# Moving elementwise work between VectorE and GpSimd, and reordering the end of a token block, in an attention + MoE kernel

## Chip, cores and metric

The kernel runs on one NeuronCore of a Trainium2 chip. The metric is the device time of one execution in microseconds (us), lower is better. Engines are named as the profile names them: PE is TensorE (PEld its weight loads), DVE is VectorE, ACT is ScalarE, POOL is GpSimd, SP is SyncE, whose queue issues nearly all DMAs.

## What is computed

Three stages run one after the other: attention with a top-32 mask, a gated MLP, and a soft mixture of eight experts. The change touches only the third:

```python
def _moe2_ref(x, w_gate, w1, w2):          # x: 2304 x 512, w1: 8 x 512 x 1024, w2: 8 x 1024 x 512
    logits = x @ w_gate
    logits = logits - logits.max()
    P = np.exp(logits)
    for _ in range(8):
        P /= P.sum(1, keepdims=True) + 1e-09
        P /= P.sum(0, keepdims=True) + 1e-09
        P *= N / E
    out = np.zeros((N, D), dtype=np.float32)
    for e in range(E):
        h = np.maximum(x @ w1[e], 0.0)
        ye = h @ w2[e]
        out += P[:, e:e + 1] * ye
```

All is float32. The kernel feeds the PE with pairs of fp32r numbers: a high part (a rounded copy, written by ACT) and a low part (the number less its high part, one two-input subtraction on DVE or POOL), so that each product is three matmuls: high x high, high x low, low x high.

## The kernel before

**Blocks and units.** The third stage cuts the 2304 tokens into three blocks of 768 (each two halves of 384), and the hidden width of each of the 8 experts into four strips: 32 units a block, 96 in all. A product of 2x2 blocks is done with seven products of sums of the quarters instead of eight (a Winograd scheme). `l1` (lines 1152 to 1187) lists the seven products of the first matrix, i0 to i6, in the order `CH` = 6, 1, 4, 2, 0, 3, 5. Each is 6 matmuls of 384 columns. ACT copies product 6 out of PSUM as `p` (line 1178), DVE adds `p` and the running sums `u`, `c` to the others (L1162, L1165), ACT takes the high part of the rectified result, `hh` (L1169), and DVE the low part `hl` (L1170). PE runs ahead by at most a step or two: product 4 is accumulated on the bank of product 6 and so waits until ACT has copied `p`, and product 2 waits in the same way for `u`.

**First block** (time 809 to 1345). After each of i1 to i6 comes `l2` of the unit before, 6 matmuls of 512 columns, whose result DVE adds to `acc` (L1214). In the same loop all that the later blocks need is made:

- `w_load` (945) loads the raw quarters of the first weight matrix of the unit after the next into `ws`, two buffers. `w_sums` (953, the operation on 957) makes four more quarters as sums and differences of them, one instruction of 128x256 in each of i3 to i6. `w_split` (964) makes the high part (ACT, 967) and the low part (POOL, 968) of one quarter for the next unit, `wa`, and stores it (970) for the later blocks.
- `w2_load`, `w2_split` (980) and `w2_more` (994) do the same for the second matrix: `wb` (984), sums `sm` (1002) on DVE, parts `sp` (1006, 1007).
- A list of `steps`, one popped in each i by `slot()` (1228): first the 16 row and column normalizations of P on DVE (`rows` and `cols`, with one matmul for each column sum), then from unit 6 on the x of blocks three and two (`x_ops`, 1021): loads, sums `xr` (1037), and 28 pairs of high part (ACT, 1047) and low part (POOL, 1048) in `both`.

**Second and third block.** Units go through `d1` (1350). Products 1 to 7 of the hidden quarters with the second matrix (`group`, 1413) run for two units at a time, as pairs, and are spread over the i of the next two units by the list `todo2`; `take` (1428) adds each into `M1` to `M7` on DVE. Their PSUM banks go by chains: 1 and 2 share one, 5 and 3, and 7, 6 and 4. `KO` = 1, 2, 5, 3, 7, 6, 4 is the order. What `d1` still owes of a unit when its seven products are done, the list `late` of four functions, is run in i0 to i3 of the next unit: t2 and then t4 (two subtractions on POOL), and the high and low parts of hidden quarters 5, 7, 6 and 4. In the second block `v_make` (1330) also makes, for every second unit, the parts of the second matrix anew from `wr`, with four sums on DVE (1338) a unit: 60 instructions.

**End of a block.** The last pair has no next unit. `finish` (1466) runs its products at once, in the order 1, 5, 3, 7, 6, 4, 2, with the `late` parts in between. `plus` (1439) adds one M to another over its two halves, and `out_cols` (1443) transposes and stores a quarter of the output. Three additions are run before it in the last unit, in i3 and i5 (`early`, 1497).

**Order.** Scheduling is manual: on each engine instructions run in the order in which the code emits them, and an instruction that waits holds everything behind it on its engine.

Of the kernel before, what the change touches and what calls it, by code (L numbers as in the profile page):

```python
# [18 lines left out]
def kernel(  # L19
# [932 lines left out]

    def w_sums(e, u, part=None):
        st = wts[e, u]
        ops = ((0, 7, 3, ALU.add), (1, 0, 6, ALU.subtract), (2, 6, 7, ALU.subtract), (5, 4, 1, ALU.subtract))
        for dst, x, y, op in ops if part is None else ops[part:part + 1]:
            nc.vector.tensor_tensor(st[:, dst], st[:, x], st[:, y], op)  # L957

# [62 lines left out]
    def x_ops(s):  # L1021
# [24 lines left out]
        def both(c, b):  # L1046
            nc.scalar.activation(xB[b][:, 0, c], cur[c][:, b], AF.Copy)
            nc.gpsimd.tensor_tensor(xB[b][:, 1, c], cur[c][:, b], xB[b][:, 0, c].bitcast(F32), ALU.subtract)

# [215 lines left out]
    for n in range(NW):  # L1265
        e, u = units[n][1:]
        ops = l1(n)
        nxt = units[n + 1][1:]
        nx2 = units[n + 2][1:]
        if n == 6:  # L1270
            steps += x_ops(2) + p_steps() + x_ops(1)
        for i, fn in enumerate(ops):
            fn()
            if n and i:
                l2(n - 1, i - 1)
            run_after()
            (w_split if n + 1 < NW else w_fetch)(*nxt, CH[i])
            if n + 2 < NW:
                if i == 0:
                    w_load(*nx2)  # L1280
                if 3 <= i:
                    w_sums(*nx2, part=i - 3)
            if stores:
                stores.pop(0)()
            if more and i != 3:
                more.pop(0)()
            if i == 3:
                w2_split(e, u)
                if n + 1 < NW:
                    w2_load(*nxt)  # L1290
                if n % 2 == 0 or n == 1:
                    more = w2_more(e, u)
            if n < 6 or i not in (3, 4):
                slot()
# [35 lines left out]
    def v_make(n, k):  # L1330
# [6 lines left out]
        for dst, x, y, op in sums:  # L1337
            nc.vector.tensor_tensor(dst, x, y, op)
        t = wk2[n % 2][k]
# [10 lines left out]
    def d1(n):  # L1350
# [50 lines left out]

        def j0():
            G_.tensor_tensor(t["t2"], t["b22"], t["t1"], ALU.subtract)
            G_.tensor_tensor(t["b21"], t["b21"], t["t2"], ALU.subtract)
            parts(5, t["t1"], G_)

        return ([i0, i1, i2, i3, i4, i5, i6],
                [j0, lambda: parts(7, t["t3"], G_), lambda: parts(6, t["t2"], G_),
                 lambda: parts(4, t["b21"], G_)])

    bank = {}

    def group(pair, k, j, first=False):

        first = first or k in (1, 5, 7)
        if first:
            bank[CHAIN[k], j] = yps.tile([128, 512], F32, name="y", tag="y")
# [9 lines left out]

    def take(pair, k, j, *dst, first=False):
        ps = group(pair, k, j, first)
        for x in dst:  # L1430
# [35 lines left out]
    def finish(s, pair, late):  # L1466
# [4 lines left out]

        run(1, 1, 2)
        late.pop(0)()
        plus(3, 6, G_)
        plus(5, 1, V)
        run(5, 5)
        for fn in late:
            fn()
        plus(3, 1, V)
        run(3, 3)  # L1480
        plus(4, 1, V)
        run(7, -3)
        run(6, 5, 3)
# [6 lines left out]
        out_cols(s, 1, 0, 0, M[4][:, 0], M[1])  # L1490
        take(pair, 2, 0, 2, first=True)
        out_cols(s, 1, 0, 1, M[4][:, 1], M[1])
        take(pair, 2, 1, 2, first=True)
        out_cols(s, 0, 0, 0, M[2][:, 0], M[5])
        out_cols(s, 0, 0, 1, M[2][:, 1], M[5], V)

    early = {3: (3, 7, G_, ALU.subtract), 5: (5, 6, G_, ALU.add)}
    todo2 = []
# [66 lines left out]
```

## Time and profile before

| | us |
|---|---|
| Median of 3 runs (2335.92 to 2339.11) | 2338.88 |
| The profiled execution's own time | 2338.49 |
| Its span, first to last instruction | 2336.7 |
| PE busy in the span | 2217.1 (95%) |
| DVE busy | 1881.6 (81%) |
| POOL busy | 1444.1 (62%) |
| ACT busy | 1193.7 (51%) |
| Mean granted PE clock | 0.979 of 2.4 GHz |

The span is made of the attention and the MLP (until about 809), the first block (809 to 1345), the second (to 1850) and the third (to the end). Busy time is the sum of instruction durations; an instruction that is held up while it runs counts as busy. "Idle before" is the time in which an engine stood still before an instruction, with what ended it.

### The profile page before, as it was taken

The page shows a single profiled execution, that of the slowest core. Times are in us where ns is not written, and L with a number is a line of the kernel's source. Part 1 is how long each engine was busy: PE and PEld are TensorE (multiplying, and loading weights), DVE is VectorE, ACT ScalarE, POOL GpSimd, SP SyncE. Part 2 cuts the span into 40 slices and gives each one's busy share as a digit, 9 for nine tenths or more (in the row PEclk, how much of TensorE's full clock was granted, in tenths as well). Part 3 has the DMA queues.
Part 4 walks back from the last instruction along what each step waited for, and adds up shares of the span by engine and source line. Part 5 has one row for each costly group of instructions (what it writes and reads, how often), then busy time and mean ns, then how long its engine had stood idle before and what let it go on. Part 6 is the DMA issues. An engine that isn't in the chain of part 4 may idle for free.

```text
span 2336.7 us, 42305 instructions
## 1 busy us (share of the span) xinstructions
PE 2217.1 (95%) x13466; PEld 2021.8 (87%) x13466; DVE 1881.6 (81%) x4556; ACT 1193.7 (51%) x2705; POOL 1444.1 (62%) x1686
## 2 busy tenths in 40 slices
PE   5897999999999989999999999999999899999998
PEld 4555898888888877888788899999999899999998
DVE  8999899999896488988798867777777667777777
ACT  8999787787776343443433343333333343332232
POOL 6889776776774254766765546666666544444444
PEclk7997999999999999999999999999999999999999
DMA  6554444544540376787767687778778887777774
GB/s 188 150 148 117 106 109 110 123 98 110 125 110 22 127 245 208 249 292 248 241 236 238 236 298 260 270 264 278 269 270 273 298 281 255 257 260 255 258 256 145
DMA packets 352062, 483.88 MB, mean 207 GB/s; under 512 B 94976, under 2 KB 161888, under 8 KB 351840
## 3 DMA queue, kind: packets, MB, share of 16 engines
q1 hardware_dynamic: 350704, 479.34, 64.2%
q8 instruction: 108, 1.77, 0.3%
q10 hardware_dynamic: 1136, 1.84, 0.2%
q14 instruction: 114, 0.93, 0.1%
HBM read 307.90 MB, written 132.43 MB: 188 GB/s over the span
## 4 chain that ended last, share of the span: by engine, by line
PE 44%; DVE 4%; DMA 2%; issue 1%; POOL 1%; ACT 1%; SPq 0%; ACTq 0%; DVEq 0%; POOLq 0%
PE l1ps L1147 21%; PE y L1423 19%; PE y L1203 3%; DMA wr<-in_moe_w_dram 1%; DVE ws L957 1%; DMA ws<-in_moe_w_dram 1%; DVE acc L1214 0%; DVE sm L1002 0%; DVE l1ps L1361 0%; ACT h L1364 0%; DVE h L1365 0%; DVE hl L1170 0%; POOL wa L968 0%; DVE l1ps L1165 0%; DVE l1ps L1358 0%
## 5 line engine op out<-in xcount | busy, mean ns | idle before, releaser
L1423 PE MATMUL y<-h,v 128*128 128x384 f32 x2688 | 550.0, 340 | 7.8 <-POOL h L1365 6.0
L1147 PE MATMUL l1ps<-xB,wa 128*128 128x384 f32 x2688 | 541.1, 338 | 5.2 <-DVE tm_u L1358 5.0
L1423 PEld LDWEIGHTS y<-h,v 128*128 128x128 f32 x2688 | 482.1, 189 | 13.3 <-POOL h L1365 6.7
L1147 PEld LDWEIGHTS l1ps<-xB,wa 128*128 128x128 f32 x2688 | 471.3, 188 | 11.3 <-DVE tm_u L1358 9.2
L968 POOL TENSOR_TENSOR wa<-ws,wa 128x256 fp32r<-128x256 f32 x217 | 169.4, 788 | 208.2 <-ACT wa L967 201.4
L1437 DVE TENSOR_TENSOR M<-y,M 128x384 f32<-128x384 f32 x424 | 229.8, 553 | 79.9 <-PE y L1423 79.3
L1147 PE MATMUL l1ps<-xAh,wa 128*128 128x384 f32 x896 | 266.3, 344 | 27.9 <-ACT p L1178 16.2
L1203 PE MATMUL y<-wb,hh 128*128 128x512 f32 x768 | 272.5, 397 | 0.0
L1365 POOL TENSOR_TENSOR h<-tm_t,h 128x384 fp32r<-128x384 f32 x192 | 197.8, 1045 | 51.2 <-ACT h L1364 51.2
L1147 PEld LDWEIGHTS l1ps<-xAh,wa 128*128 128x128 f32 x896 | 165.2, 188 | 51.7 <-ACT p L1178 25.1
L1365 POOL TENSOR_TENSOR h<-tm_b,h 128x384 fp32r<-128x384 f32 x128 | 132.5, 1039 | 123.4 <-ACT h L1364 117.1
L315 POOL TENSOR_TENSOR low<-s_sb 128x288 int32<-128x288 int32 x144 | 117.6, 817 | 98.1 <-ACT s_sb L293 96.4
L338 DVE MAX8 tkv<-rest 128x8 f32<-128x288 f32 x432 | 175.2, 448 | 0.0
L1203 PEld LDWEIGHTS y<-wb,hh 128*128 128x128 f32 x768 | 145.9, 190 | 25.6
L1364 ACT ACTIVATE h<-tm_b 128x384 fp32r<-128x384 f32 x128 | 67.1, 524 | 188.2 <-DVE tm_b L1361 182.1
L289 PE MATMUL sps<-kst,qst 128*128 128x288 f32 x640 | 131.4, 334 | 33.3 <-DVE top L322 32.2
L1214 DVE SCALAR_TENSOR_TENSOR acc<-y,P,acc 128x512 f32<-128x512 f32 x168 | 123.7, 742 | 47.6 <-PE y L1203 42.9
L1341 POOL TENSOR_TENSOR v<-wr,v 128x256 fp32r<-128x256 f32 x105 | 80.3, 765 | 129.2 <-ACT v L1340 114.4
L1364 ACT ACTIVATE h<-l1ps 128x384 fp32r<-128x384 f32 x128 | 62.8, 490 | 184.0 <-DVE l1ps L1361 182.8
L1203 PE MATMUL y<-wb,hl 128*128 128x512 f32 x384 | 152.8, 398 | 0.0
L1147 PE MATMUL l1ps<-xAl,wa 128*128 128x384 f32 x448 | 150.5, 336 | 0.0
L289 PEld LDWEIGHTS sps<-kst,qst 128*128 128x128 f32 x640 | 100.9, 203 | 56.5 <-DVE top L322 44.8
(205 smaller groups left out, 5344.8 us busy)
## 6 DMA issues: line engine op xcount, KB each, us to landing
wa<-wk SPq DMA_DIRECT2D x448, 256.0 KB, 3.3
v<-vk SPq DMA_DIRECT2D x343, 256.0 KB, 3.7
wk<-wa SPq DMA_DIRECT2D x224, 256.0 KB, 2.6
vk<-v SPq DMA_DIRECT2D x105, 256.0 KB, 2.6
vk<-sp SPq DMA_DIRECT2D x68, 256.0 KB, 3.0
raw<-in_moe_w_dram SPq DMA_DIRECT2D x32, 512.0 KB, 3.8
ws<-in_moe_w_dram SPq DMA_DIRECT2D x128, 128.0 KB, 2.5
ws<-in_moe_w_dram SPq DMA_DIRECT2D x32, 512.0 KB, 4.6
```

What stands on the lines that cost most here:

```text
L289: nc.tensor.matmul(ps[:, e, 0:SH], lhs, kst[p, part][:, hh, SH * e:SH * e + SH], start=(n == 0), stop=(n == len(terms) - 1))
L315: nc.gpsimd.tensor_tensor(low_sb[st][:, j].bitcast(I32), x[:, 0:SH], x[:, SH:S], ALU.add)
L338: nc.vector.max(vt[:, j, c:c + 8], x[:, j])
L968: eng.tensor_tensor(t[:, 1], st[:, c], t[:, 0].bitcast(F32), ALU.subtract)
L1147: nc.tensor.matmul(ps, lhs[:, kc], rhs[:, kc], start=(first and k_ == 0), stop=(k_ == 3 * KH - 1), skip_group_check=True)
L1203: nc.tensor.matmul(ps, lhs[:, m, h, o:o + 128], rhs[:, m], start=(k_ == 0), stop=(k_ == 5))
L1214: nc.vector.scalar_tensor_tensor(a, ps, P[:, i, e:e + 1], a, op0=ALU.mult, op1=ALU.add)
L1341: nc.gpsimd.tensor_tensor(t[:, 1], src, t[:, 0].bitcast(F32), ALU.subtract)
L1364: nc.scalar.activation(h[k][:, 0], src, AF.Copy)
L1365: low = lambda: eng.tensor_tensor(h[k][:, 1], src, h[k][:, 0].bitcast(F32), ALU.subtract)
L1423: nc.tensor.matmul(ps, w[:, a, 128 * j:128 * j + 128], h[:, b], start=(first and q_ == 0), stop=(q_ == 5), skip_group_check=True)
L1437: nc.vector.tensor_tensor(m, ps, m, ALU.add)
```

## The change

Four parts:

1. `w_sums` takes an engine, and the first block's loop gives it POOL: 120 sums (30 units, 4 each) go from DVE to POOL. The two calls ahead of the loop stay on DVE.
2. In `both`, the 28 low parts of x go from POOL to DVE.
3. In `v_make`, the 60 sums go from DVE to POOL.
4. `late` is cut in another way: the part of quarter 5 first, then t2 with the part of 7, then t4 with the part of 6. `finish` runs 1, 3, 5, 7, 6, 4, 2; product 1 goes into two banks of its own (`far`, from the pool of the first matrix's products), and product 2 is accumulated on them; the additions among the M are rearranged.

```diff
-    def w_sums(e, u, part=None):
+    def w_sums(e, u, part=None, eng=None):
...
-            nc.vector.tensor_tensor(st[:, dst], st[:, x], st[:, y], op)
+            (eng or V).tensor_tensor(st[:, dst], st[:, x], st[:, y], op)
...
-            nc.gpsimd.tensor_tensor(xB[b][:, 1, c], cur[c][:, b], xB[b][:, 0, c].bitcast(F32), ALU.subtract)
+            nc.vector.tensor_tensor(xB[b][:, 1, c], cur[c][:, b], xB[b][:, 0, c].bitcast(F32), ALU.subtract)
...
-                    w_sums(*nx2, part=i - 3)
+                    w_sums(*nx2, part=i - 3, eng=G_)
...
-            nc.vector.tensor_tensor(dst, x, y, op)
+            nc.gpsimd.tensor_tensor(dst, x, y, op)
...
-        def j0():
+        def t2():
             G_.tensor_tensor(t["t2"], t["b22"], t["t1"], ALU.subtract)
+
+        def t4():
             G_.tensor_tensor(t["b21"], t["b21"], t["t2"], ALU.subtract)
-            parts(5, t["t1"], G_)
...
-                [j0, lambda: parts(7, t["t3"], G_), lambda: parts(6, t["t2"], G_),
-                 lambda: parts(4, t["b21"], G_)])
+                [lambda: parts(5, t["t1"], G_), lambda: (t2(), parts(7, t["t3"], G_)),
+                 lambda: (t4(), parts(6, t["t2"], G_)), lambda: parts(4, t["b21"], G_)])
...
-        if first:
+        if far:
+            bank[CHAIN[k], j] = lps.tile([128, 512], F32, name="z", tag="l1")
+        elif first:
...
-        run(1, 1, 2)
-        late.pop(0)()
-        plus(3, 6, G_)
-        plus(5, 1, V)
-        run(5, 5)
+        for j in range(2):
+            take(pair, 1, j, 1, far=True)
         for fn in late:
             fn()
+        for j in range(2):
+            take(pair, 3, j, 3, first=True)
+        run(5, 5, 3)
+        plus(4, 1, G_)
+        plus(5, 1, V)
+        run(7, -3)
         plus(3, 1, V)
-        run(3, 3)
-        plus(4, 1, V)
-        run(7, -3)
         run(6, 5, 3)
...
-        take(pair, 2, 0, 2, first=True)
+        take(pair, 2, 0, 2)
...
-        take(pair, 2, 1, 2, first=True)
+        take(pair, 2, 1, 2)
...
-    early = {3: (3, 7, G_, ALU.subtract), 5: (5, 6, G_, ALU.add)}
+    early = {3: (3, 7, G_, ALU.subtract), 4: (5, 6, G_, ALU.add), 5: (3, 6, G_, ALU.add)}
```

On ACT and on SP no instruction changes its place. Three places of the order, with the change's line numbers where rows are new:

POOL in the first unit of the first block, i3 to i6 (`ws` holds the raw quarters and their sums):

```order
 L968 TENSOR_TENSOR wa_10853<-ws_10371,wa_10853 128x256
+L957 TENSOR_TENSOR ws_10814<-ws_10814 128x256
 L984 TENSOR_TENSOR wb<-ws_10803,wb 128x1024
 L968 TENSOR_TENSOR wa_10875<-ws_10371,wa_10875 128x256
+L957 TENSOR_TENSOR ws_10814<-ws_10814 128x256
 L968 TENSOR_TENSOR wa_10899<-ws_10371,wa_10899 128x256
+L957 TENSOR_TENSOR ws_10814<-ws_10814 128x256
 L1007 TENSOR_TENSOR sp<-sm_10881,sp 128x256
 L968 TENSOR_TENSOR wa_10922<-ws_10371,wa_10922 128x256
+L957 TENSOR_TENSOR ws_10814<-ws_10814 128x256
```

Each sum now stands behind a low part, the first ahead of the long `wb` part of the second matrix.

DVE at the first of four runs of seven low parts of x (`xr` is x, `xB` its parts), i5 of one unit to i1 of the next:

```order
-L957 TENSOR_TENSOR ws_12167<-ws_12167 128x256
+L1048 TENSOR_TENSOR xB_10796<-xr,xB_10796 128x384
 L1165 TENSOR_TENSOR l1ps<-l1ps,u_12187 128x384
 L1214 SCALAR_TENSOR_TENSOR acc<-y,P,acc 128x512
 L1170 SCALAR_TENSOR_TENSOR hl<-l1ps,hh 128x384
-L957 TENSOR_TENSOR ws_12167<-ws_12167 128x256
+L1048 TENSOR_TENSOR xB_10793<-xr,xB_10793 128x384
+L1048 TENSOR_TENSOR xB_10795<-xr,xB_10795 128x384
 L1162 TENSOR_TENSOR u_12364<-l1ps,p_12343 128x384
-L1214 SCALAR_TENSOR_TENSOR acc<-y,P,acc 128x512 x2
-L1170 SCALAR_TENSOR_TENSOR hl<-l1ps,hh 128x384
+L1214 SCALAR_TENSOR_TENSOR acc<-y,P,acc 128x512
```

Sums are gone; the low parts stand where POOL had them in time, each behind the unit's own `hl`.

DVE in `finish` of the third block, before (`M5_16787` and the like are M5, M1, M3, M4; `y` banks 26643 and 26651 hold products 5 and 3, 26683 and 26691 product 7):

```order
L1441 TENSOR_TENSOR M5_16787<-M5_16787,M1_16785 128x384 x2
L1437 TENSOR_TENSOR M5_16787<-y_26643,M5_16787 128x384
L1437 TENSOR_TENSOR M5_16787<-y_26651,M5_16787 128x384
L1441 TENSOR_TENSOR M3_16788<-M3_16788,M1_16785 128x384 x2
L1437 TENSOR_TENSOR M3_16788<-y_26643,M3_16788 128x384
L1437 TENSOR_TENSOR M3_16788<-y_26651,M3_16788 128x384
L1441 TENSOR_TENSOR M4_16791<-M4_16791,M1_16785 128x384 x2
L1433 TENSOR_TENSOR M3_16788<-M3_16788,y_26683 128x384
L1433 TENSOR_TENSOR M3_16788<-M3_16788,y_26691 128x384
```

The same place in the change (`y` banks 26661 and 26670 hold product 5):

```order
L1440 TENSOR_TENSOR M5_16787<-y_26661,M5_16787 128x384
L1440 TENSOR_TENSOR M3_16788<-y_26661,M3_16788 128x384
L1440 TENSOR_TENSOR M5_16787<-y_26670,M5_16787 128x384
L1440 TENSOR_TENSOR M3_16788<-y_26670,M3_16788 128x384
L1444 TENSOR_TENSOR M5_16787<-M5_16787,M1_16785 128x384 x2
L1436 TENSOR_TENSOR M3_16788<-M3_16788,y_26683 128x384
L1436 TENSOR_TENSOR M3_16788<-M3_16788,y_26691 128x384
L1444 TENSOR_TENSOR M3_16788<-M3_16788,M1_16785 128x384 x2
L1440 TENSOR_TENSOR M5_16787<-y_26683,M5_16787 128x384
```

The subtraction of product 7 (L1433 before, L1436 now), which must be over before product 6 can be accumulated on its bank, stands behind one pair of M additions instead of three since product 1; the pair for M3 follows it and the one for M4 is on POOL.

## Rows read from the trace of the kernel before

**Rows 1.** By stretch: us, busy PE PEld DVE ACT POOL, PEclk, DMA share, GB/s.

```profile
810.00:960.00 150.00, 133.46 (x647) 115.44 (x646) 131.38 (x240) 62.75 (x147) 86.11 (x92) 0.98 0.67 229
960.00:1190.00 230.00, 216.47 (x1049) 187.66 (x1048) 197.23 (x298) 92.60 (x224) 154.45 (x160) 0.99 0.74 257
1190.00:1320.00 130.00, 128.95 (x638) 113.81 (x637) 115.00 (x173) 50.79 (x122) 75.68 (x81) 1.00 0.71 242
```

**Rows 2.** The same view, inside the second block.

```profile
1440.00:1800.00 360.00, 358.24 (x2016) 352.35 (x2016) 274.28 (x528) 135.75 (x324) 234.56 (x252) 1.00 0.79 270
```

**Rows 3.** Waits from 840 to 1350: waiter <- awaited: us, times, longest.

```profile
PEld l1ps L1147 <- ACT p L1178: 21.7, 20, 2.4
```

**Rows 4.** Timeline of VectorE around one stop: start, us, what.

```profile
859.63 0.90 DVE L957 TENSOR_TENSOR ws<-ws 128x256 f32<-128x256 f32 x1
860.46 0.96 DVE L1002 TENSOR_TENSOR sm<-sm,ws 128x256 f32<-128x256 f32 x1
861.34 0.55 DVE L1165 TENSOR_TENSOR l1ps<-l1ps,u 128x384 f32<-128x384 f32 x1
```

**Rows 5.** Timeline of ScalarE, same place.

```profile
861.93 0.49 ACT L1169 ACTIVATE hh<-l1ps 128x384 fp32r<-128x384 f32 x1 [2.19 <-DVE l1ps L1165]
...
862.93 0.48 ACT L1178 ACTIVATE p<-l1ps 128x384 f32<-128x384 f32 x1
```

**Rows 6.** Timeline of TensorE, same place.

```profile
863.46 0.44 PE L1147 MATMUL l1ps<-xAh,wa 128*128 128x384 f32 x1 [1.79 <-ACT p L1178]
```

**Rows 7.** VectorE by group, 810 to 1340: xcount | busy us, mean ns.

```profile
L957 DVE TENSOR_TENSOR ws<-ws 128x256 f32<-128x256 f32 x120 | 125.8, 1048 | 18.9 <-DMA ws<-in_moe_w_dram 17.3 <-POOL wa L968 1.5
...
L1170 DVE SCALAR_TENSOR_TENSOR hl<-l1ps,hh 128x384 fp32r<-128x384 f32 x93 | 50.9, 548 | 7.1 <-ACT hh L1169 7.1
...
L1170 DVE SCALAR_TENSOR_TENSOR hl<-c,hh 128x384 fp32r<-128x384 f32 x31 | 22.5, 725 | 1.3 <-ACT hh L1169 1.3
...
L1037 DVE TENSOR_TENSOR xr<-xr 128x384 f32<-128x384 f32 x16 | 13.8, 867 | 0.7 <-DMA xr<-x2s 0.7
```

**Rows 8.** GpSimd by group, same stretch.

```profile
L968 POOL TENSOR_TENSOR wa<-ws,wa 128x256 fp32r<-128x256 f32 x217 | 169.4, 788 | 208.2 <-ACT wa L967 201.4 <-DMA vk<-sp 2.7 <-DMA ws<-in_moe_w_dram 2.7
...
L984 POOL TENSOR_TENSOR wb<-ws,wb 128x1024 fp32r<-128x1024 f32 x31 | 74.9, 2417 | 4.0 <-ACT wb L983 3.4 <-DMA ws<-in_moe_w_dram 0.6
...
L1048 POOL TENSOR_TENSOR xB<-xr,xB 128x384 fp32r<-128x384 f32 x28 | 31.2, 1114 | 0.0
```

**Rows 9.** Waits of SyncE's DMA queue, 840 to 1340.

```profile
SPq L970 <- POOL wa L968: 234.5, 137, 5.2
```

**Rows 10.** Waits of ScalarE, 1380 to 1860.

```profile
ACT v L1340 <- DVE wr L1338: 38.6, 13, 3.1
```

**Rows 11.** Timeline of TensorE, end of the second block.

```profile
1823.44 4.45 PE L1423 MATMUL y<-h,v 128*128 128x384 f32 x22
1832.60 10.30 PE L1423 MATMUL y<-h,v 128*128 128x384 f32 x44 [4.71 <-POOL h L1365]
```

**Rows 12.** Timeline of GpSimd, same place.

```profile
1826.40 1.97 POOL L1441 TENSOR_TENSOR M<-M,M 128x384 f32<-128x384 f32 x2
...
1829.02 1.30 POOL L1403 TENSOR_TENSOR tm_t<-tm_b,tm_t 128x384 f32<-128x384 f32 x1
...
1831.56 0.99 POOL L1365 TENSOR_TENSOR h<-tm_t,h 128x384 fp32r<-128x384 f32 x1
```

**Rows 13.** Timeline of TensorE, end of the third block.

```profile
2309.18 3.31 PE L1423 MATMUL y<-h,v 128*128 128x384 f32 x18
...
2315.27 1.66 PE L1423 MATMUL y<-h,v 128*128 128x384 f32 x8 [1.30 <-POOL h L1365]
...
2322.84 2.38 PE L1423 MATMUL y<-h,v 128*128 128x384 f32 x12 [0.55 <-DVE M L1433]
```

**Rows 14.** Timeline of VectorE, same place.

```profile
2317.78 2.68 DVE L1441 TENSOR_TENSOR M<-M,M 128x384 f32<-128x384 f32 x2
...
2321.31 1.01 DVE L1441 TENSOR_TENSOR M<-M,M 128x384 f32<-128x384 f32 x2
```

More of the change, by code (lines that the diff above doesn't have):

```diff
@@ L1400, in i6, with group @@
             V.tensor_tensor(t["t3"], t["b22"], ps, ALU.subtract)
-        def j0():
+        def t2():
             G_.tensor_tensor(t["t2"], t["b22"], t["t1"], ALU.subtract)
+        def t4():
             G_.tensor_tensor(t["b21"], t["b21"], t["t2"], ALU.subtract)
-            parts(5, t["t1"], G_)
         return ([i0, i1, i2, i3, i4, i5, i6],
-                [j0, lambda: parts(7, t["t3"], G_), lambda: parts(6, t["t2"], G_),
-                 lambda: parts(4, t["b21"], G_)])
+                [lambda: parts(5, t["t1"], G_), lambda: (t2(), parts(7, t["t3"], G_)),
+                 lambda: (t4(), parts(6, t["t2"], G_)), lambda: parts(4, t["b21"], G_)])
     bank = {}
-    def group(pair, k, j, first=False):
+    def group(pair, k, j, first=False, far=False):
         first = first or k in (1, 5, 7)
-        if first:
+        if far:
+            bank[CHAIN[k], j] = lps.tile([128, 512], F32, name="z", tag="l1")
+        elif first:
             bank[CHAIN[k], j] = yps.tile([128, 512], F32, name="y", tag="y")
@@ L1426, in group, with take @@
         return ps
-    def take(pair, k, j, *dst, first=False):
-        ps = group(pair, k, j, first)
+    def take(pair, k, j, *dst, first=False, far=False):
+        ps = group(pair, k, j, first, far)
         for x in dst:
```

## Prediction

> **What bounds the kernel now.** I first read the busy time by stretch. Inside the second block PE is busy 358.24 of 360.00 us [rows 2]: it is the bound there, and work of other engines is hidden. In the first block it isn't quite: from 810 to 1320 PE stands still 150.00 - 133.46 = 16.5, 230.00 - 216.47 = 13.5 and 130.00 - 128.95 = 1.1 us [rows 1], 31.1 us together, and the granted clock is below full, 0.98 and 0.99: 0.02 x 150 + 0.01 x 230 = 5.3 us of full clock are missing.
>
> The waits say who stops PE: weight loads of the first product wait 21.7 us in 20 stops on ACT's copy `p` [rows 3]. ACT is not the cause. At one stop DVE runs a weight sum (0.90 us) and a sum `sm` (0.96) before its addition for the last product of the unit, which starts at 861.34 [rows 4]; ACT waited 2.19 us for that, and its copy `p`, second next but one, starts at 862.93 [rows 5]; PE stood still 1.79 us until 863.46 [rows 6]. So a DVE that comes late, through extra work put between the steps that PE needs, is what bounds this block.
>
> DVE is busy 131.38 + 197.23 + 115.00 = 443.6 of 510 us there, 87%; POOL 86.11 + 154.45 + 75.68 = 316.2, 62% [rows 1]. Busy share alone does not tell: in the last stretch DVE is at 88% and PE loses only 1.1 us, since the extra work there is the same in each unit. In the other two it comes in bursts: normalizations, then the sums of x.
>
> **Part 1, the sums of weight quarters.** 120 sums leave DVE: 125.8 us, 1.048 each [rows 7]. POOL gets them at the price of its low part of the same shape, 0.788 [rows 8]: 94.6 us. The bounds are 0.60 (a quarter of the 2.417 of a part four times as wide) and 1.05 (the DVE mean). The POOL row with the same shape and kind of operands is nearest, so I take it. What waits behind a sum on POOL is the low part of the next quarter, needed by PE only in the next unit (32 units from 809 to 1345, some 16.8 us each), and its store, for which SP's queue waits [rows 9]. A sum is used by ACT in the next unit at the earliest, four steps later. I price this wait at nothing; without that cover see the second rival.
>
> By the Trainium skill ("GPSIMD Engine Reference", 4.1 Engine selection) two-input elementwise work is about twice as slow on GpSimd as on VectorE. By that rule on DVE's 1.048 a sum would take 2.1 us, POOL would have 316 - 31 + 252 = 537 us of work in 510 and be the bound. The row speaks against it: POOL does the same shape in 0.788, less than DVE's mean, because a DVE operation with two SBUF inputs is held up beside a busy POOL.
>
> **Part 2, the low parts of x.** 28 leave POOL, 31.2 us [rows 8]. On DVE a two-input operation of this shape took 0.725 (`hl` from `c`) to 0.867 (`xr`); 1.114, POOL's own time, is the upper bound. I take 0.867, the same shape, two SBUF inputs and the same part of the block: 24.3 us. DVE also waits for ACT's high part, which stands behind other copies: between nothing and about 1.0 us, the time from `hh` to `p` in [rows 5] with two copies between. For the sum I take nothing for that wait itself, since ACT is then no longer late, and account for the bursts below.
>
> DVE comes to 443.6 - 125.8 + 24.3 = 342 us, 67%; POOL to 316.2 - 31.2 + 94.6 = 379.6, 74%. That leaves DVE below the 88% at which the regular last stretch ran almost without stops. Of PE's 31.1 us I keep 3.5 in the first stretch (column sums that PE itself waits for, and units with normalizations and `sm` together) and 5 in the second: four runs of seven low parts, one to two stops of the present size each, 1.2 us a run. That choice is mine; the rows bound it only by 0 and 31.1. Saved: 31.1 - 8.5 = 22.6. The missing 5.3 us of clock are time at 1.2 instead of 2.4 GHz; matmuls are slow right behind a long stop [rows 11], so fewer stops should give some back. I take half: 2.6. Bounds 0 and 5.3.
>
> **Part 3, sums of the second matrix.** 60 sums go to POOL, at 0.788 some 47 us over the second block, where POOL is busy 234.56 of 360 [rows 2]. PE idles 1.8 us in these 360, so at most 2.4 in the block can be won. ACT waited 38.6 us, 13 times, for these sums on DVE [rows 10]; on POOL they can run as soon as their inputs are there. I take 0 for the block, and count what it does at its end there.
>
> **Part 4, the ends of blocks.** In the second block PE stops 4.71 us until 1832.60, for the low part of quarter 5 that POOL starts at 1831.56 [rows 11, 12]. The 44 matmuls after it take 10.30 us, 0.234 each, against 3.31 / 18 = 0.184 where nothing holds them up [rows 13]: 2.2 us more. In the change t2 and t4 (from 1829.02 to 1831.56, 2.5 us) go behind that part, but an M3 pair of 1.97 [rows 12] comes ahead of it, so it is ready 0.5 earlier; and product 3's 12 matmuls, 2.2 us, run before PE needs it. That is 2.7 us by which product 6 starts earlier. If the sum for quarter 3, no longer held up behind DVE's additions (longest wait 3.1 [rows 10]), lets POOL's whole queue come 2 us earlier, it is 4.7. I take 4.0. Bounds: 0.5, if the wait for product 7's subtraction takes the place, and 6.9, stop and slow matmuls together.
>
> In the third block PE stops 1.30 us for the same low part, and product 6 starts at 2322.84 after DVE's subtraction of product 7 [rows 13]. In the change: 18 matmuls from 2309.18 (the loop's last 6 and product 1) end at 2312.5, and 24 more, products 3 and 5 without a stop, at 2316.9; DVE's two last additions from PSUM at 0.55 (as `hl` from a bank [rows 7]) at 2318.0; then one M pair, 2.68 beside a busy POOL and 1.01 beside an idle one [rows 14], of which I take 2.2 since POOL has parts left, and one subtraction, 0.55. Product 6 can start at 2320.75, 2.1 us earlier. Bounds 1.6 and 3.3. PE, through with product 7 by 2319.1, still waits about 1.7 us there.
>
> **Sum.** 2338.5 (the profiled execution) - 22.6 - 2.6 - 4.0 - 2.1 = 2307.2; the median of the runs is 0.4 above that execution: **2307.6 us**. The forecast's own ends: with all of PE's stops and clock and the upper ends of part 4 gone, 2338.9 - 31.1 - 5.3 - 6.9 - 3.3 = 2292.3; with half the stops and the lower ends, 2338.9 - 15.6 - 0 - 0.5 - 1.6 = 2321.2.
>
> **Rivals.**
>
> *DVE's other work gets slower.* DVE's operations with two SBUF inputs are those that suffer beside POOL: `hl` from `c` takes 0.725, from a PSUM bank 0.548 [rows 7], and a sum has 1.048. In the block 31 `hl`, 68 `sm`, 16 `xr` and 28 low parts stay. If each waits half a POOL operation more, 143 x 0.4 = 57 us come back: DVE at 399 us, 78%, half of the gain lost. Late POOL work would do the same: SP's queue already waits 234.5 us, 137 times, for low parts [rows 9], and the raw weights are loaded by that queue. A third of the stops saved, 10.4, with 1 of clock and 4 at the ends: 2338.9 - 15.4 = 2323.5. For it: POOL's share rises to 74%. Against: the operations that leave are the ones that suffered most.
>
> The Trainium skill ("Perfetto Trace Analysis", Optimizing Scalar/DVE Operations) warns that the two engines share a port and that moving work between them might not help. The rows agree that they get in each other's way; what the warning would make of the time is this rival.
>
> *Low parts of x stop PE: slower.* DVE now stands still at each low part until ACT's copy is there, and the next product's addition, `u` or `c`, is queued behind it. If each part costs PE its own 0.867 and half the wait, 0.5, it is 28 x 1.37 = 38.4 us against 31.3 won: 2346.0. It decides from 31.3 / 28 = 1.1 us a part. For it: POOL was never idle before these parts, which shows ACT's copy in time only for a late POOL [rows 8]. Against: between the product that `u` is made from and the one that needs it PE has one product of the first matrix and two of the second, which takes up the delay of one part.
>
> *It doesn't do what it says.* PE's stops are bound to ACT's own order, which stays, and the ends trade one wait for another: 2338.9, 2335 to 2341.
>
> **Chances.** Forecast 0.65, first rival 0.23, slower 0.07, no effect 0.05. Range 2293 to 2328: the forecast's ends and the first rival. 0.2%, 4.7 us, is about what a measurement of this kernel can tell from no change: faster by more 0.88 (forecast and first rival), within 0.05, slower 0.07.
>
> **What would show it.** Right: from 810 to 1320 PE idle under 12 us with DVE near 67% and POOL near 74%; stops on `p` gone but for the low parts' units; sums on POOL near 0.79, low parts on DVE near 0.87; the stop at the second block's end under 3.5 us; product 6 of the third held by DVE, not POOL. Wrong: sums over 1 us on POOL, ACT waiting for POOL's sums, new PE stops behind xB on DVE, or a first block that is not at least 10 us shorter.

## The result, and the profile after

The changed kernel takes 2310.05 us (median) against 2338.99 for the kernel before on the same chip; the ratio is 0.9876, 95% interval 0.9857 to 0.9895. One of its four executions took 2717.38 us at a granted clock of 0.745; it is in that median and not in the ratio, and the median of the other three is 2308.97. The forecast was 2307.6, range 2293 to 2328. The profiled execution spans 2307.1 us, against 2336.7. TensorE's timelines of these two executions give where the 29.6 us between the spans went. The marks are the first product of `l1`, the first one that reads `xB`, the last one ahead of a block's end, and the first one of the next block:

| stretch, us | before | after | difference |
|---|---|---|---|
| up to the first `l1` product | 807.68 | 807.77 | 0.1 |
| first block | 549.90 | 527.96 | -21.9 |
| second block, loop | 465.68 | 460.86 | -4.8 |
| its end, up to the third block's first product | 26.87 | 24.79 | -2.1 |
| third block, loop | 458.87 | 458.88 | 0.0 |
| its end, up to the last instruction | 27.70 | 26.84 | -0.9 |

The total came out as forecast, but by other terms. The busy time by stretch of the changed kernel (us, then PE, PEld, DVE, ACT, POOL, the granted clock), to be read against [rows 1] and [rows 2]:

```profile
810.00:960.00 150.00, 141.35 (x695) 123.56 (x694) 127.90 (x225) 66.01 (x156) 114.58 (x127) 0.99 0.71 243
960.00:1190.00 230.00, 222.38 (x1095) 197.32 (x1095) 187.07 (x277) 97.91 (x237) 181.58 (x198) 0.99 0.77 267
1190.00:1320.00 130.00, 130.00 (x651) 116.96 (x650) 91.27 (x142) 52.81 (x123) 99.82 (x113) 1.00 0.72 244
1440.00:1800.00 360.00, 359.73 (x2042) 358.03 (x2041) 261.20 (x488) 139.97 (x329) 270.12 (x305) 1.00 0.80 275
```

From 810 to 1320 PE stands still 8.65 + 7.62 + 0 = 16.3 us, where it was 31.1 and under 12 was to show the forecast right. DVE is busy 406.2 of 510 us, 80%, where 67% was forecast; POOL 396.0, 78%, where 74% was. A part of both is the window: the block is shorter, so more of its work lies in the same 510 us. The waits of the same block:

```profile
POOL ws L957 <- DMA ws<-in_moe_w_dram: 27.6, 19, 4.8
...
PEld l1ps L1147 <- ACT p L1178: 9.8, 8, 2.2
PEld l1ps L1147 <- DVE u L1162: 9.0, 8, 1.5
```

The stops on `p` fell from 21.7 us in 20 [rows 3] to 9.8 in 8. Those that are left stand behind other extra work of VectorE: the sums `sm`, and in the middle of the block the low parts of x. One of them, on VectorE, ScalarE and TensorE (to be read like [rows 4] to [rows 6]):

```profile
989.87 0.90 DVE L1002 TENSOR_TENSOR sm<-sm,ws 128x256 f32<-128x256 f32 x1
990.69 1.09 DVE L1048 TENSOR_TENSOR xB<-xr,xB 128x384 fp32r<-128x384 f32 x1
991.71 0.55 DVE L1165 TENSOR_TENSOR l1ps<-l1ps,u 128x384 f32<-128x384 f32 x1
...
992.29 0.49 ACT L1169 ACTIVATE hh<-l1ps 128x384 fp32r<-128x384 f32 x1 [1.91 <-DVE l1ps L1165]
...
994.24 0.44 PE L1147 MATMUL l1ps<-xAh,wa 128*128 128x384 f32 x1 [1.59 <-ACT p L1178]
```

The groups of VectorE from 810 to 1320 show what took the room (compare [rows 7]):

```profile
L1170 DVE SCALAR_TENSOR_TENSOR hl<-l1ps,hh 128x384 fp32r<-128x384 f32 x94 | 51.5, 547 | 8.0 <-ACT hh L1169 7.9
L1170 DVE SCALAR_TENSOR_TENSOR hl<-c,hh 128x384 fp32r<-128x384 f32 x31 | 42.5, 1372 | 1.3 <-ACT hh L1169 1.3
...
L1048 DVE TENSOR_TENSOR xB<-xr,xB 128x384 fp32r<-128x384 f32 x28 | 23.4, 834 | 1.5 <-ACT xB L1047 1.2
...
L1037 DVE TENSOR_TENSOR xr<-xr 128x384 f32<-128x384 f32 x16 | 16.2, 1018 | 0.0
```

GpSimd's, same stretch (compare [rows 8]):

```profile
L957 POOL TENSOR_TENSOR ws<-ws 128x256 f32<-128x256 f32 x120 | 101.0, 842 | 32.7 <-DMA ws<-in_moe_w_dram 28.6 <-DMA wk<-wa 3.9
...
L984 POOL TENSOR_TENSOR wb<-ws,wb 128x1024 fp32r<-128x1024 f32 x32 | 77.6, 2424 | 0.8 <-ACT wb L983 0.8
```

The moved operations cost about what was assumed: a sum 0.842 on POOL (0.788 taken), a low part 0.834 on DVE (0.867 taken). What grew is work that the change doesn't touch: `hl` from `c`, with both inputs in SBUF, from 0.725 to 1.372, while the same operation from a PSUM bank stayed at 0.547.

The end of the second block on TensorE, against [rows 11]:

```profile
1804.71 3.80 PE L1426 MATMUL y<-h,v 128*128 128x384 f32 x20 [1.78 <-POOL h L1365]
1809.80 2.38 PE L1426 MATMUL y<-h,v 128*128 128x384 f32 x12 [1.29 <-DVE M L1436]
1813.33 0.55 PE L1450 MATMUL otp<-ident,M 128*128 128x128 f32 x3 [1.15 <-DVE M L1440]
```

The stop of 4.71 became 1.78, and the slow matmuls behind it are gone (20 in 3.80, 0.190 each); but two new stops of over 1 us stand behind it, on DVE. In the third block it is one, against [rows 13]:

```profile
2283.60 6.47 PE L1426 MATMUL y<-h,v 128*128 128x384 f32 x36
2293.27 2.38 PE L1426 MATMUL y<-h,v 128*128 128x384 f32 x12 [3.20 <-DVE M L1436]
```

VectorE there, against [rows 14]:

```profile
2288.95 3.80 DVE L1444 TENSOR_TENSOR M<-M,M 128x384 f32<-128x384 f32 x2
2292.68 1.01 DVE L1436 TENSOR_TENSOR M<-M,y 128x384 f32<-128x384 f32 x2
```

And GpSimd:

```profile
2288.96 1.01 POOL L1365 TENSOR_TENSOR h<-tm_b,h 128x384 fp32r<-128x384 f32 x1
2289.93 1.94 POOL L1444 TENSOR_TENSOR M<-M,M 128x384 f32<-128x384 f32 x2
```

The pair on M5 was taken at 2.2 us and lasts 3.80: it begins with GpSimd's low part and gets through only when GpSimd's pair on M4 has ended at 2291.87. The subtraction that PE waits for is queued behind it.

### The profile page after: what moved, and what is told of

Read it like the earlier page. It is cut to its first block, busy times and chain, and to the rows that moved or that the text cites. A ratio compares the mean times of both kernels' runs of the same rounds, so it can differ in the third digit from the quotient of the medians.

```text
span 2307.1 us, 42178 instructions
## 1 busy us (share of the span) xinstructions
PE 2202.1 (95%) x13466; PEld 2021.3 (88%) x13466; DVE 1807.0 (78%) x4400; ACT 1198.1 (52%) x2705; POOL 1550.9 (67%) x1842
## 4 chain that ended last, share of the span: by engine, by line
PE 74%; DVE 10%; POOL 5%; ACT 3%; DMA 3%; issue 2%; SPq 2%; ACTq 0%; POOLq 0%; DVEq 0%
PE l1ps L1147 27%; PE y L1426 19%; PE y L1203 9%; PE abps L628 7%; PE x2ps L645 4%; PE sps L289 2%; PE tx L427 2%; DVE tkv L338 2%; PE tx L398 2%; DMA kst<-kt 1%; DVE sm L1002 1%; DVE rest L343 1%; DVE G L500 1%; POOL low L327 1%; DVE hl L1170 1%
## 5 line engine op out<-in xcount | busy, mean ns | idle before, releaser
L1426 PE MATMUL y<-h,v 128*128 128x384 f32 x2640 | 537.1, 339 | 6.7 <-DVE M L1436 4.5
L1426 PEld LDWEIGHTS y<-h,v 128*128 128x128 f32 x2640 | 472.4, 188 | 9.2 <-DVE M L1436 5.1
L1365 DVE TENSOR_TENSOR h<-l1ps,h 128x384 fp32r<-128x384 f32 x128 | 71.1, 555 | 104.9 <-ACT tm_b L1393 64.0
```

The costliest lines, as they stand in the source:

```text
L1365: low = lambda: eng.tensor_tensor(h[k][:, 1], src, h[k][:, 0].bitcast(F32), ALU.subtract)
L1426: nc.tensor.matmul(ps, w[:, a, 128 * j:128 * j + 128], h[:, b], start=(first and q_ == 0), stop=(q_ == 5), skip_group_check=True)
```

## The experiments

How finely they can be read: kernels whose first block is the same code gave 549.90, 549.43 and 550.96 (the order of before), and 527.96, 529.10, 526.56, 526.58 and 526.59 (that of the change); the third block's end in the order of before took 27.70 to 27.75 in seven kernels. Executions of one kernel spread over 2 to 13 us, and the stretch up to the first `l1` product alone, the same code in all, took 804.76 to 812.05. So whole times are given as ratios with their intervals, and the stretches, each from the one profiled execution, are read beside them.

**Each part alone, on the kernel before.** The sums of weight quarters:

```diff
-                    w_sums(*nx2, part=i - 3)
+                    w_sums(*nx2, part=i - 3, eng=G_)
```

> The kernel before with one part of the change: the 120 sums of weight quarters on GpSimd, the 28 low parts of x still there as well. Theory (the gain of the first block is these sums leaving VectorE): the first block, from TensorE's first l1 product at 807.7 to the first product that reads xB, is 18 to 24 us shorter than before's 549.9, VectorE's other operations with two inputs in SBUF get slower (low parts from c from 725 to over 1200 ns), and the second and third blocks keep before's lengths to 1 us; whole time 2315 to 2321. Rival (GpSimd can't hold both the sums and the low parts of x, and the exchange of both is what gains): the block gains less than 10 us, TensorE waits for wa or xB, whole time over 2328.

Measured: ratio 0.9918 (0.9901 to 0.9934), 2317.95 us. The first block took 534.75, 15.2 less, below what the theory gave but far from the rival; low parts from `c` took 1361 ns. The second block's loop, which the edit doesn't touch, also came out shorter, 460.27. The theory of the main gain holds, with less than its range; that the other blocks keep their lengths fell.

The low parts of x:

```diff
-            nc.gpsimd.tensor_tensor(xB[b][:, 1, c], cur[c][:, b], ...
+            nc.vector.tensor_tensor(xB[b][:, 1, c], cur[c][:, b], ...
```

> The kernel before with the 28 low parts of x on VectorE alone, the sums still there as well. Theory (VectorE's load is what stops TensorE in the first block): 28 operations of about 0.85 us in about a quarter of the block's units add 24 us to VectorE where it has little room, and half of it or so reaches TensorE: the block is 5 to 20 us longer, whole time 2344 to 2358. Rival (low parts of x are a gain or nothing by themselves, since they lie in VectorE's waits and free GpSimd): the block changes by less than 3 us, whole time 2336 to 2342.

Measured: ratio 0.9997 (0.9986 to 1.0009), first block 551.85. The rival holds: 21 us of operations more on VectorE (its busy time from 810 to 1320 rose from 443.6 to 458.6) cost TensorE nothing that can be told from the spread. So VectorE's load by itself does not decide.

The sums of `v_make`:

```diff
-            nc.vector.tensor_tensor(dst, x, y, op)        # v_make
+            nc.gpsimd.tensor_tensor(dst, x, y, op)
```

> The kernel before with the 60 sums of v_make on GpSimd alone. The prediction put this at 0 (2338.9); the changed kernel's second block was however 4.8 us shorter in its loop, more than expected. Theory (VectorE's sums held up TensorE now and then in the second block's loop): the second block's loop, from its first product to the last l1 product before its end, is 2.5 to 5 us shorter, whole time 2333.5 to 2336.5. Rival (the loop's gain comes from the new order of the late low parts): the loop keeps its length to 1 us, whole time 2338 to 2340.

Measured: ratio 0.9965 (0.9952 to 0.9978), 2330.24 us, more than the theory gave. The loop of the second block is 458.86, as long as the third block's, which makes nothing anew. Its end also fell, from 26.87 to 23.40. TensorE's waits in the loop, in the kernel before:

```profile
PEld l1ps L1147 <- DVE tm_u L1358: 6.5, 10, 1.4
PEld y L1423 <- DVE M L1437: 2.9, 10, 0.3
```

and with the sums on GpSimd, where the second group is gone:

```profile
PEld l1ps L1147 <- DVE tm_u L1358: 2.8, 3, 1.6
```

The third block's loop of the kernel before has 2.7 us in 3 of these. What the sums did on VectorE shows in the kernel before, near the end of the second block. VectorE had no idle time there:

```profile
1813.16 1.02 DVE L1437 TENSOR_TENSOR M<-y,M 128x384 f32<-128x384 f32 x2
1814.09 0.42 DVE L1338 TENSOR_TENSOR wr<-wr 128x256 f32<-128x256 f32 x1
```

and ScalarE, in order, stood at the copy that reads the sum, with the high parts of hidden quarters behind it:

```profile
1811.00 0.49 ACT L1369 ACTIVATE tm_p<-l1ps 128x384 f32<-128x384 f32 x1 [0.17 <-PE l1ps L1147]
1814.59 0.42 ACT L1340 ACTIVATE v<-wr 128x256 fp32r<-128x256 f32 x1 [3.10 <-DVE wr L1338]
1814.92 0.92 ACT L1364 ACTIVATE h<-tm_t 128x384 fp32r<-128x384 f32 x2
```

With the sums on GpSimd no wait of ScalarE for them is left in that loop, and TensorE's stop for quarter 5's low part at the block's end is 1.53 instead of 4.71:

```profile
1821.81 1.68 PE L1423 MATMUL y<-h,v 128*128 128x384 f32 x8 [1.53 <-POOL h L1365]
```

The new order alone (all sums and low parts where the kernel before has them):

> The kernel before with the new order alone: the late low parts in four steps, the end of the two blocks, the early pairs of M. Theory (what the changed kernel's trace shows at the two ends is this part's): TensorE's stop of 4.7 us at the end of the second block falls below 2 and the clock stays up there, that end is 2 to 4 us shorter, the end of the third block 0.5 to 1.5 us, and the pair of M5 takes over 3 us beside GpSimd as in the changed kernel; first block unchanged; whole time 2333 to 2336.5. Rival (the end of the second block needs VectorE's sums gone from the loop as well): ends together less than 1.5 us shorter, whole time 2337.5 to 2340.

Measured: ratio 1.0033 (1.0022 to 1.0044), 2346.94 us: slower by some 8 us, which neither theory said. Its profile is of its fastest execution (2339.12) and shows 0.6 us of that; where the rest lies stays open. First block 550.96, loop 467.09, the ends 26.48 and 28.39. The stop at the second end fell to 2.52, but a second one of 3.00 on the subtraction took its place.

**Parts of the change.** The low parts of x back on GpSimd:

> The changed kernel with the 28 low parts of x back on GpSimd. Theory (once the sums are on GpSimd, GpSimd has no room for the low parts too, and VectorE has): the first block, 528.0 us in the changed kernel, is 4 to 9 us longer, as the sums alone on GpSimd gave 534.8 there; GpSimd's operations in the block's first half wait less and TensorE stops for xB or wa; second and third block as in the changed kernel to 2 us; whole time 2313 to 2319. Rival (where the low parts run makes no difference, as it made none of its own to the kernel before, 551.9 against 549.9): the block is within 2 us of 528.0, whole time 2307 to 2312.

Measured: ratio 0.9904 (0.9887 to 0.9921), 2316.25 us. The first block is 530.88, 2.9 longer than the changed kernel's, less than expected; with the sums alone, the same code in this block, it was 534.75. So the low parts gain some 2 to 8 us (530.88 and 534.75 against 526.56 to 529.10), but only once the sums have left VectorE. POOL is then busy 410.9 of 510 us with the low parts and 396.0 without; that this is the reason is likely, not shown. The second block's loop, the same code as the changed kernel's, took 459.09 instead of 460.86. The ends, also the same code, took 26.88 and 28.42 instead of 24.79 and 26.84: at the second TensorE waited 1.96 us for a load of `v`, at the third the clock fell (last section).

The pair on M5 behind the subtraction:

```diff
-        plus(5, 1, V)
         run(7, -3)
+        plus(5, 1, V)
```

> The changed kernel with VectorE's pair on M5 (M5 += M1) issued behind the subtraction that reads product 7, not ahead of it. Theory (TensorE's stop of 3.20 us before product 6 at the end of the third block is that subtraction queued behind a pair that GpSimd holds up, 3.80 us): the stop falls below 1 us and the first transposes come 1.5 to 3 us earlier; at the end of the second block 0.5 to 1.5 us; whole time 2305 to 2308.5. Rival (VectorE's pairs are still due before the transposes, and the stop only moves to there): the first transposes at the end of the third block stand within 0.5 us of 15.24 after the last l1 product; whole time 2309 to 2311.

Measured: ratio 0.9876 (0.9859 to 0.9894), 2309.63 us, no change. The stop before product 6 is gone and the first transposes come 13.99 after the last `l1` product, not 15.24: so far the theory, a little under its 1.5. But TensorE now waits at the transposes:

```profile
2287.35 8.58 PE L1426 MATMUL y<-h,v 128*128 128x384 f32 x48
2298.00 0.55 PE L1450 MATMUL otp<-ident,M 128*128 128x128 f32 x3 [2.07 <-DVE M L1440]
2298.46 2.29 PE L1426 MATMUL y<-h,v 128*128 128x384 f32 x6
```

and the six matmuls behind take 2.29, not 1.30: the granted clock of these 2.29 us is 0.50, the level of 1.2 GHz. The end is 27.41, against 26.84, in an execution that was the slowest of its four. The rival had the mechanism, a stop that only moves, and the whole time; its 0.5 us at the transposes was too narrow.

The change without its new order:

> The changed kernel without its new order: sums of weight quarters and of v_make on GpSimd, low parts of x on VectorE, late low parts and the ends of blocks as in the kernel before. Theory (the order gains nothing once v_make's sums are on GpSimd: it cost 1.4 us in the second block's loop when put alone, and v_make's sums alone gave the end of that block 23.40 where the changed kernel has 24.79): first block 526 to 530, second block's loop 458.5 to 460, its end 23 to 24.5, third block's end 27.7; whole time 2304 to 2309, that is 0 to 5 us below the changed kernel. Rival (the order is worth the 6 us of the prediction at the ends): whole time 2313 to 2317.

Measured: ratio 0.9854 (0.9838 to 0.9870), 2304.15 us, against the changed kernel's 0.9876 and 2310.05. The two intervals overlap, but the stretches say which way: first block 526.56, loop 458.82, ends 23.43 and 27.72, each where the theory put it. By these two traces the order gains 0.9 at the third end and loses 1.4 at the second and 2.0 in the loop. The loss at the second end is firm: 24.79 to 26.88 in the three kernels with the split, new ends and `v_make`'s sums on GpSimd, 23.40 to 23.43 in the four with these sums there and before's order. The gain at the third is not: 26.84 here, but 28.42 with the low parts back on GpSimd and 28.39 with the order alone, both over before's 27.70.

The late low parts split in the last unit of a block alone, with the pair later:

```diff
+        if (n + 1) % NW:
+            return ([i0, ..., i6],
+                    [lambda: (t2(), t4(), parts(5, t["t1"], G_)), lambda: parts(7, t["t3"], G_),
+                     lambda: parts(6, t["t2"], G_), lambda: parts(4, t["b21"], G_)])
```

> The changed kernel with two edits: the pair on M5 behind the subtraction, and the late low parts in the new four steps in the last unit of a block alone, in before's steps in all others. Theory (the new steps cost the second block's loop its 2 us, 460.9 against 458.9 with v_make's sums alone, since the additions t2 and t4 come a slot later each and ScalarE waits for them in order): second block's loop 458.5 to 459.5, ends as with the pair alone; whole time 2302 to 2306.5, the fastest of the kernels so far. Rival (the loop's 2 us come from something else, such as the time at which wr lands): loop over 460.3, whole time as with the pair alone, 2305 to 2308.5.

Measured: ratio 0.9855 (0.9839 to 0.9872), 2304.47 us. The loop is 458.94, where the theory put it. The seven kernels with `v_make`'s sums on GpSimd and without this split in the loop lie at 458.80 to 458.94, the three with it at 459.09, 460.86 and 461.23: the split lets the loop lose up to 2.4 us, and in one execution it lost next to nothing.

**What holds VectorE up.** In the changed kernel an operation with two inputs in SBUF stands until GpSimd's has ended. GpSimd:

```profile
1002.01 2.41 POOL L984 TENSOR_TENSOR wb<-ws,wb 128x1024 fp32r<-128x1024 f32 x1
```

VectorE:

```profile
1003.43 1.41 DVE L1170 SCALAR_TENSOR_TENSOR hl<-c,hh 128x384 fp32r<-128x384 f32 x1
```

`hl` ends at 1004.84, 0.42 after `wb` at 1004.42. The 32 of these `hl` in the first block are all of this kind or free: seven take 0.55 to 0.56 us, and the other 25, from 0.56 to 2.65 long, each end 0.41 to 0.43 behind the end of a GpSimd operation. A VectorE that is only slowed down beside GpSimd would not end in step with it. The next three kernels try this.

The first starts from the kernel with before's order and cuts `wb` in two. In that kernel VectorE's group was

```profile
L1170 DVE SCALAR_TENSOR_TENSOR hl<-c,hh 128x384 fp32r<-128x384 f32 x32 | 37.5, 1172 | 1.3 <-ACT hh L1169 1.3
```

and the edit is:

```diff
-        nc.gpsimd.tensor_tensor(hl[:, 1], st, hl[:, 0].bitcast(F32), ALU.subtract)
+        for m in range(2):
+            nc.gpsimd.tensor_tensor(hl[:, 1, m], st[:, m], hl[:, 0, m].bitcast(F32), ALU.subtract)
```

> The kernel with before's order (first block 526.6) with GpSimd's low part of wb, one operation of 128x1024 (2.46 us), made in two of 128x512. Theory (a VectorE operation with both inputs in SBUF stands still until the GpSimd operation that is running has ended, however long that is): the low parts from c, 1172 ns, which are issued while wb's operation runs, fall to 700 to 1000 ns, while wb's two halves take 2.5 to 2.9 us together; the first block is within 3 us of 526.6. Rival (both engines run slower side by side, whatever the length of an operation): the low parts from c stay at 1100 to 1250 ns. Whole time within 3 us of 2304 either way.

Measured: ratio 0.9839 (0.9824 to 0.9853), 2299.05 us. VectorE's group, and GpSimd's:

```profile
L1171 DVE SCALAR_TENSOR_TENSOR hl<-c,hh 128x384 fp32r<-128x384 f32 x32 | 30.7, 960 | 1.2 <-ACT hh L1170 1.2
```

```profile
L985 POOL TENSOR_TENSOR wb<-ws,wb 128x512 fp32r<-128x512 f32 x64 | 86.1, 1366 | 0.8 <-ACT wb L983 0.8
```

1172 ns fell to 960 by halving an operation on another engine, although that engine now works 7.5 us longer (78.6 to 86.1): the hold, not a slower rate. The first block is 520.42, 6.1 shorter, twice what either side allowed, so some of the gain that the first block fell short of had been lost here.

The second starts from the kernel with the split in the last unit alone and the pair on M5 later:

```diff
-        plus(4, 1, G_)
         run(7, -3)
         plus(5, 1, V)
         plus(3, 1, V)
         run(6, 5, 3)
+        plus(4, 1, V)
```

> The kernel with late low parts split in the last units alone and the pair on M5 later, with one edit: the pair on M4 (M4 += M1) goes from GpSimd to VectorE, behind the additions of product 6. Theory (VectorE's two pairs ahead of the transposes, 3.13 and 4.25 us at the two ends, are held up by GpSimd's last low parts and by that pair; without the pair they take 2.0 to 3): TensorE's stop before the first transposes falls from 2.07 and 3.16 us to 0.5 to 1.8, the half clock behind it goes, and the ends take 24.5 to 26 (third block, 27.39) and 22.5 to 24 (second block, 25.20); whole time 2300 to 2303.5. Rival (GpSimd's late low parts alone hold up VectorE's pairs, and the half clock stays): the ends within 0.7 us of 27.39 and 25.20, whole time 2303 to 2306.

Measured: ratio 0.9838 (0.9824 to 0.9853), 2298.94 us. The ends are 22.20 and 24.67 long. VectorE's two pairs at the third end, and TensorE's stop, first in the kernel that it starts from:

```profile
2284.70 3.12 DVE L1448 TENSOR_TENSOR M<-M,M 128x384 f32<-128x384 f32 x4
...
2288.35 0.55 PE L1454 MATMUL otp<-ident,M 128*128 128x128 f32 x3 [2.06 <-DVE M L1444]
```

and then here:

```profile
2285.29 1.96 DVE L1448 TENSOR_TENSOR M<-M,M 128x384 f32<-128x384 f32 x4
```

```profile
2287.77 0.55 PE L1454 MATMUL otp<-ident,M 128*128 128x128 f32 x3 [0.89 <-DVE M L1444]
2288.24 1.31 PE L1430 MATMUL y<-h,v 128*128 128x384 f32 x6
```

Four additions in 1.96 us, where they had taken 3.12 (and in the changed kernel two of them 3.80); the stop is short and the clock stays up. GpSimd's last operation ends at 2284.64, ahead of them: putting *more* work on VectorE made it faster, because GpSimd was quiet. Both ends are now shorter than in before's order (23.40 and 27.70).

The third starts again from the kernel with before's order:

```diff
-        nc.gpsimd.tensor_tensor(hl[:, 1], st, ...)              # wb's low part
+        after.append(lambda: nc.vector.tensor_tensor(hl[:, 1], st, ...))
-            nc.vector.tensor_tensor(sm[k], x, y, op)
+            nc.gpsimd.tensor_tensor(sm[k], x, y, op)
```

> The kernel with before's order with a second exchange in the first block: wb's low part (32 operations, 78.6 us on GpSimd) on VectorE, a step later, and the 68 sums sm (65 us on VectorE) on GpSimd. Theory (what counts is how much of VectorE's time goes to operations with two inputs in SBUF beside a busy GpSimd): wb takes 1.2 to 2 us on VectorE, sm 0.75 to 0.9 on GpSimd, both engines lose 5 to 25 us of busy time, low parts from c fall below 900 ns, and the first block is 2 to 8 us shorter than 526.6; whole time 2296 to 2302. Rival (an operation of over 1.2 us in VectorE's queue makes the sums behind it late, which TensorE waits for): the first block is 2 to 15 us longer; whole time 2306 to 2319.

Measured: ratio 0.9833 (0.9817 to 0.9850), 2298.38 us; first block 519.78. From 810 to 1320:

```profile
810.00:1320.00 510.00, 497.72 (x2481) 441.62 (x2480) 373.47 (x609) 219.16 (x518) 382.66 (x473) 1.00 0.76 256
```

```profile
L984 DVE TENSOR_TENSOR wb<-ws,wb 128x1024 fp32r<-128x1024 f32 x32 | 42.7, 1335 | 0.0
```

Both engines lost work at once, DVE 404.7 to 373.5 and POOL 394.8 to 382.7: 128x1024 takes 1.34 on VectorE and 2.46 on GpSimd. Low parts from `c` took 1042 ns, over the 900 expected: 28 of the 32 lasted 1.08 to 1.11 us and ended 0.41 to 0.42 behind the end of a GpSimd operation, now of 128x256. The hold is there without `wb` too.

**Together:**

> The two things that gained, together: the second exchange in the first block (low parts of wb on VectorE, sums sm on GpSimd) and the ends of blocks with the pair on M5 later and the pair on M4 on VectorE. Theory (first block and ends don't touch each other): first block 518 to 522, second block's loop 458.5 to 459.5, its end 22 to 22.6, third block's end 24.5 to 25; whole time 2290 to 2295. Rival (a gain in one place is given back in another, by the clock or by the DMA queue): whole time 2296 to 2300.

Measured: ratio 0.9809 (0.9796 to 0.9822), 2294.11 us, faster than both kernels. First block 521.26, loop 458.90, ends 21.20 (under the 22 expected) and 24.69.

## Why the prediction was right, and where it was not

**The first block** was forecast to gain 22.6 and 2.6 of clock, and gained 21.9. The mechanism was right: sums between the steps that TensorE needs were what made VectorE late, and moving them alone gave 15.2. The term that was mis-sized is what was kept of PE's stops: 8.65 and 7.62 us are left in the first two stretches, where 3.5 and 5 were put, so the stops gave 14.8 and not 22.6. The clock gave some 1.5, from 0.98 to 0.99 in 150 us. The other 5.6 of the 21.9 lie in time that the profile counts as busy and stood in no term, so that the block's gain came out so near was in part luck.

VectorE's load came to 80% for 67%, partly by the window and partly since the operations that stay were left at their old durations. The first rival had put 399 us for that, and 406.2 were measured; but its consequence, that half the gain is lost, did not follow: the waits of the block show no stop of TensorE for `hl` from `c`, the operation that grew most (20.0 of busy time, 42.5 against 22.5). It stands in VectorE's queue all the same, and the hold did cost something: 6.1 us with `wb` in halves. That the load is why stops were left is not shown; the low parts alone raised it and cost nothing.

By the Trainium skill ("SBUF — State Buffer", Who interferes with whom) a VectorE operation with two SBUF inputs contends with a GpSimd operation that reads SBUF, and the lock between them is exclusive. The traces agree (the ends 0.41 to 0.43 us behind a GpSimd operation's; 1172 to 960 ns with the halves of `wb`). The rule of the Trainium skill that the prediction weighed ("GPSIMD Engine Reference", 4.1 Engine selection: about twice as slow) did not bear out for the sums of weight quarters: one took 0.842 us, against 1.048 on VectorE. It does where VectorE isn't held: a sum of `v_make` of the same 128x256 took 0.42 there, at 1814.09 in the kernel before, and the operation of 128x1024 1.34, against 2.46 on GpSimd.

**The low parts of x** cost no time that shows: the second rival, slower, is refuted by the part alone (0.9997), and with the sums gone they are worth 2 to 8 us. But its mechanism is in the trace: the stop of 1.59 us at 994.24 stands behind a low part, a new stop behind `xB` as the prediction's list of wrong signs has it.

**The sums of `v_make`** were taken at 0 in the block, with 2.4 at most, since PE "idles 1.8 us in these 360", and at some 1.3 of the 4.0 at its end. This step failed. Alone they are worth 8 us (0.9965): 6.8 in the loop, 3.5 at its end. A hint of the price stood in the trace of before: the second block's loop takes 465.68 and the third's, with as many matmuls, 458.87. The busy share did not show it in full; the ends of matmuls are modelled in it. [Rows 10] had a part of the cause; it was put down as harmless. In the changed kernel ScalarE still waits for these sums, 24.6 us in 13 times, now on GpSimd, and the loop is shorter all the same.

**The ends of blocks** were forecast at -4.0 and -2.1, mostly by the new order. This failed too. The changed kernel's second end gained 2.1 and its third 0.9, but `v_make`'s sums alone give the second 3.5, and the order alone makes the kernel slower (1.0033). Two terms were wrong: the pair beside GpSimd, 3.80 for 2.2, and the wait for product 7's subtraction, which the prediction had only in the lower bound of the second end and which came about (1.29 us there; at the third 3.20, where some 1.7 was put). The split of the late low parts costs up to 2.4 in the loop, a cost that the prediction left out. The order's idea was not wrong in itself: with the pairs kept out of GpSimd's way the ends came to 22.20 and 24.67.

So 2307.6 came near 2310.05 because errors cancelled. With the kernel without the new order as the measure, the stretches give 3.3 us too much gain forecast for the first block (25.2 against 21.9), 9.0 too little for `v_make` (1.3 against 6.9 + 3.4), and 7.3 too much for the order (2.7 + 2.1 forecast, 2.0 + 1.4 - 0.9 = 2.5 lost): -31.3 + 3.3 - 9.0 + 7.3 = -29.7, as the spans differ. Still open is why the second block's loop was shorter also with the weight sums alone, 460.27 with `v_make`'s sums on VectorE; in the other three kernels with these sums there it was 465.68 to 467.09. TensorE's waits for `tm_u` in it were 3.7 us in 4, against 6.5 in 10 in the kernel before, so the sums do not stop TensorE in every unit, and the 6.8 us are not a fixed price. No run isolates it.

## What to carry to other kernels

Look for the same loop without the suspect in another stage of the trace and subtract, before you believe a busy share: here that pointed at the 7 us that the moved sums were worth. When two engines exclude each other, count which operations are issued beside which, not how long each takes alone: splitting or removing the other engine's long operation can be worth more than moving work. And test the parts of a change one by one even where its total comes out as forecast: here one of four was a loss as it stood, and a few small edits made a gain of it.

## What the runs showed of the chip

A VectorE operation can be held for more than one GpSimd operation: the first addition on M5, alone, in VectorE's timeline of the changed kernel

```profile
2288.95 3.33 DVE L1444 TENSOR_TENSOR M<-M,M 128x384 f32<-128x384 f32 x1
```

ended at 2292.28. GpSimd's low part had ended at 2289.97 and its two queued additions went through first, until 2291.87. In the first block it was nearly always one.

The same stop did not always cost the clock. TensorE stood 3.20 us before product 6 at the third end in the changed kernel and the 12 matmuls behind took 2.38, at a granted clock of 1.00; with the low parts back on GpSimd, the same code there:

```profile
2296.32 3.81 PE L1426 MATMUL y<-h,v 128*128 128x384 f32 x12 [3.19 <-DVE M L1436]
```

3.81 us, at a granted clock of 0.57: most of them ran at 1.2 GHz, not 2.4. So taking such a stop away can be worth more than the stop, and moving it may gain nothing, as with the pair on M5.
